# Running the first block's FFN as two half-batch passes, with their own loads, and products of a zero tile before them

## Chip, cores, metric

The kernel runs on one core of a Trainium2 chip. The metric is the device time of one execution in microseconds (us), the median of several runs. The span of a profile is about 2 us shorter, since it runs from the first to the last instruction. All runs quoted were classed fast, but for one run of the kernel before (246.25 us, named below), which was classed slow and is in no ratio; a one-core program has no second die to compare with.

## The reference, cut to what matters

A decayed linear attention over 4 batches, 8 heads, 768 positions and 64 dimensions (q, k, v), followed by a gated FFN on the 3072 x 512 result:

```python
# attention, block by block, with a state kv_state carried from block to block
out[:, :, sl] = intra + inter
kv_state = lam_block * kv_state + einsum('bhsd,bhse->bhde', kb_dec, vb)
...
gate = 1.0 / (1.0 + np.exp(-(x @ w_gate)))     # 512 -> 1536
val  = x @ w_val                               # 512 -> 1536
return (gate * val) @ w_out                    # 1536 -> 512
```

All inputs are float32 in HBM. The kernel converts them to bf16 while it loads them.

## The kernel before

The 768 positions are worked in six blocks of 128. A block is 4 batches x 128 positions = 512 tokens. TensorE gets a hand-made list of pieces. The ones that matter here are:

```python
def load(n, what, b0, b1):    # q, k, v of block n, batches b0..b1, by a queue that POOL fills
    ...
def load_gv(i, w):            # one sixth (256 columns) of w_gate and of w_val
    fs = slice(i * w, (i + 1) * w)
    nc.gpsimd.dma_start(out=WG[:, :, fs], in_=wg_r[:, :, fs])
    nc.gpsimd.dma_start(out=WV[:, :, fs], in_=wv_r[:, :, fs])

# piece_t: transposes of q and k     piece_s: scores     piece_m: score x mask -> MT (DVE)
# piece_a: products of MT and v, then the copy PSUM -> XT (XT is the FFN's input)
# piece_c: update of the state Sb

def piece_gv(n, ft):          # one of 12 column tiles of gate and value, 512 tokens
    for mt in range(NMT):     # 4 products, 512 columns
        nc.tensor.matmul(gp, lhsT=WG[:, mt, fs], rhs=x[:, mt, :], ...)
    nc.scalar.activation(sg, gp, AF.Sigmoid)
    for mt in range(NMT):
        nc.tensor.matmul(vp, lhsT=WV[:, mt, fs], rhs=x[:, mt, :], ...)
    nc.vector.tensor_mul(HT[n, ft], sg, vp)
...
piece_t(0, 0)                 # block 0: all attention first
piece_s(0, [0]); piece_m(0, 0)    # (one call per line in the kernel)
...
piece_a(0, [3])
units = gv[0] + gv[1][:4] + po[0] + gv[1][4:] + po[1]      # then the FFN
place(1, (2, 3), (8, 10), (9, 11), (11, 11))  # block 1's attention between block 0's FFN units
```

The four pairs of `place` are the FFN units after which the state update, the transposes, the scores and the products of v are put, one number for each pair of batches. The first loads, in queue order, are q and k of batches 0-1, q and k of batches 2-3, v of both halves, then the weight pieces 0 to 4, block 1's first q and k, and weight piece 5. From block 2 on, q and k are transposed by DMA instead of TensorE. SyncE issues those transposes in one instruction order with the output stores.

Of the kernel before, what the change touches and what calls it, by code (L numbers as in the profile page):

```python
# [8 lines left out]
FP32 = mybir.dt.float32  # L9
# [7 lines left out]
def kernel(  # L17
# [11 lines left out]
    nc = tc.nc  # L29
# [41 lines left out]
    def load(n, what, b0, b1):  # L71
        sl = slice(n * C, (n + 1) * C)
        for c in what:
            lst, src = {"q": (Q, q), "k": (K, k), "v": (V, v)}[c]
            if n not in lst:
                lst[n] = qkv.tile([128, B, H, D], BF16, tag=c + "b", name=c + "b")
            t = lst[n]
            nc.gpsimd.dma_start(  # L78
                out=t[:, b0:b1],
                in_=src[b0:b1, :, sl, :].rearrange("b h s d -> s (b h) d"))  # L80

    def load_gv(i, w):
# [3 lines that stand above are left out]
# [3 lines left out]
        nc.gpsimd.dma_start(out=WO[:, fs, :], in_=wo_r[:, fs, :])  # L89

    nc.scalar.preload_act_table_set("natural_log_exp_and_others")
    ident = const.tile([128, 128], BF16, tag="ident")
    make_identity(nc, ident)
    jn = const.tile([128, 2], FP32, tag="jn")
    ip1 = const.tile([128, C], FP32, tag="ip1")
    tri = const.tile([128, C], FP32, tag="tri")

    load(0, "q", 0, 2)
    for i, base in enumerate((-1, C - 1)):
        nc.gpsimd.iota(jn[:, i:i + 1], pattern=[[0, 1]], base=base, channel_multiplier=-1,  # L100
                       allow_small_or_imprecise_dtypes=True)
    load(0, "k", 0, 2)
    make_upper_triangular(nc, tri, val=1.0, diag=True)
    load(0, "q", 2, 4)
    nc.gpsimd.iota(ip1, pattern=[[1, C]], base=1, channel_multiplier=0,
                   allow_small_or_imprecise_dtypes=True)
    load(0, "k", 2, 4)
    load(0, "v", 0, 2)
    load(0, "v", 2, 4)


    Sb = stp.tile([128, B, HP, 128], BF16, tag="Sb", name="Sb")
    nc.vector.memset(Sb, 0.0)

    lnl = const.tile([128, H], FP32, tag="lnl")
    nc.scalar.activation(lnl, lam_bc, AF.Ln)
# [32 lines left out]
    def piece_t(n, bp):  # L149
        if n > 1:  # L150
            QS[n, bp] = trsb.tile([128, 2, HP, C], BF16, tag="QS", name="QS")
            nc.vector.tensor_tensor(out=QS[n, bp], in0=QR[n][:, 2 * bp:2 * bp + 2],  # L152
                                    in1=lamq.unsqueeze(1).to_broadcast([128, 2, HP, C]), op=ALU.mult)
            return
        tq = ps_at.tile([128, 2, HP, C], BF16, name="tq", tag="ps")
        tk = ps_at.tile([128, 2, HP, C], BF16, name="tk", tag="ps")
        for i in range(2):
            for hp in range(HP):
                nc.tensor.transpose(tq[:, i, hp, :], Q[n][:, 2 * bp + i, 2 * hp:2 * hp + 2, :], ident)  # L159
        QS[n, bp] = trsb.tile([128, 2, HP, C], BF16, tag="QS", name="QS")  # L160
        nc.vector.tensor_tensor(out=QS[n, bp], in0=tq,
                                in1=lamq.unsqueeze(1).to_broadcast([128, 2, HP, C]), op=ALU.mult)
        for i in range(2):
            for hp in range(HP):
                nc.tensor.transpose(tk[:, i, hp, :], K[n][:, 2 * bp + i, 2 * hp:2 * hp + 2, :], ident)  # L165
        KS[n, bp] = trsb.tile([128, 2, HP, C], BF16, tag="KS", name="KS")
        nc.scalar.copy(KS[n, bp], tk)  # L167
# [3 lines left out]
    def piece_s(n, bs):  # L171

        for b in bs:
            bp, i = b // 2, b % 2
            sp = [ps_at.tile([128, HP, C], FP32, name=f"sp{u}", tag="ps") for u in range(2)]
            for hp in range(HP):
                for u in range(2):
                    us = slice(u * 64, (u + 1) * 64)
                    nc.tensor.matmul(sp[u][:, hp, :], lhsT=KS[n, bp][us, i, hp, :],  # L179
                                     rhs=QS[n, bp][us, i, hp, :],  # L180
                                     start=(hp == 0), stop=(hp == HP - 1), skip_group_check=True)
            SP[n, b] = sp

    def piece_m(n, b):
        MT[n, b] = mtp.tile([128, 2, HP, C], BF16, tag="MT", name="MT")
        for u in range(2):
            nc.vector.tensor_tensor(out=MT[n, b][:, u], in0=SP[n, b][u], in1=mask[:, u], op=ALU.mult)  # L187

    def piece_a(n, bs):
        for b in bs:  # L190
            OP[n, b] = ps_at.tile([128, HP, C], FP32, name="op", tag="ps")
            for hp in range(HP if n > 0 else 0):
                nc.tensor.matmul(OP[n, b][:, hp, :], lhsT=Sb[:, b, hp, :],  # L193
                                 rhs=QS[n, b // 2][:, b % 2, hp, :],
                                 start=(hp == 0), stop=False, skip_group_check=True)
        for b in bs:
            for hp in range(HP):
                for u in range(2):
                    us = slice(u * 64, (u + 1) * 64)
                    nc.tensor.matmul(OP[n, b][us, hp, :], lhsT=V[n][:, b, 2 * hp + u, :],  # L200
                                     rhs=MT[n, b][:, u, hp, :],
                                     start=(n == 0 and hp == 0), stop=(hp == HP - 1),
                                     skip_group_check=True)
        if n not in XT:
            XT[n] = xtp.tile([128, NMT, B, C], BF16, tag="XT", name="XT")
        for b in bs:
            nc.scalar.copy(XT[n][:, :, b, :], OP[n, b])  # L207

    def make_kd(n):
        KD[n] = kdp.tile([128, B, H, D], BF16, tag="kd", name="kd")  # L210
        nc.gpsimd.tensor_tensor(  # L211
            out=KD[n], in0=K[n],
            in1=kds.unsqueeze(1).unsqueeze(3).to_broadcast([128, B, H, D]), op=ALU.mult)

    def piece_c(n, bs):
        for b in bs:
# [18 lines left out]

    HT = {}

    def piece_gv(n, ft):
        fs = slice(ft * 128, (ft + 1) * 128)
        x = XT[n].rearrange("p m b c -> p m (b c)")  # L240
        gp = ps_ff.tile([128, TCH], FP32, name="gp", tag="ff")
        for mt in range(NMT):
            nc.tensor.matmul(gp, lhsT=WG[:, mt, fs], rhs=x[:, mt, :],  # L243
                             start=(mt == 0), stop=(mt == NMT - 1))
        sg = htp.tile([128, TCH], BF16, tag="sg", name="sg", bufs=3)
        nc.scalar.activation(sg, gp, AF.Sigmoid)  # L246
        vp = ps_ff.tile([128, TCH], FP32, name="vp", tag="ff")
        for mt in range(NMT):
            nc.tensor.matmul(vp, lhsT=WV[:, mt, fs], rhs=x[:, mt, :],  # L249
                             start=(mt == 0), stop=(mt == NMT - 1))  # L250
        HT[n, ft] = htp.tile([128, TCH], BF16, tag="ht", name="ht", bufs=2 * NFT)
        nc.vector.tensor_mul(HT[n, ft], sg, vp)  # L252

    def piece_po(n, tt):
        po = ps_ff.tile([128, DM], FP32, name="po", tag="ff")
# [5 lines left out]
        nc.sync.dma_start(out=out[tt * S + n * C:tt * S + (n + 1) * C, :], in_=ob)  # L261


    for i in range(5):
        load_gv(i, DFF // 6)
    make_kd(0)
    load(1, "qk", 0, 2)
    load_gv(5, DFF // 6)
    load(1, "qk", 2, 4)
    load(1, "v", 0, 2)  # L270
    load(1, "v", 2, 4)
# [1 line left out]
        load_wo(i, NFT // 3)  # L273
    make_kd(1)


    piece_t(0, 0)
    piece_s(0, [0])
    piece_m(0, 0)
    piece_s(0, [1])  # L280
    piece_m(0, 1)
    piece_t(0, 1)
    piece_s(0, [2])
    piece_m(0, 2)
    piece_a(0, [0])
    piece_s(0, [3])
    piece_m(0, 3)
    piece_a(0, [1])
    piece_a(0, [2])
    piece_a(0, [3])  # L290

    gv = [[lambda n=n, ft=ft: piece_gv(n, ft) for ft in range(NFT)] for n in range(NSTEP)]
    po = [[lambda n=n, tt=tt: piece_po(n, tt) for tt in range(B)] for n in range(NSTEP)]

    units = gv[0] + gv[1][:4] + po[0] + gv[1][4:] + po[1]
    for n in range(2, NSTEP):
        units += gv[n] + po[n]
    start = {0: 0, 1: NFT}
    for n in range(2, NSTEP):
        start[n] = n * (NFT + B)  # L300
    after = [[] for _ in units]

    def place(n, c, t, s, a):


        for bp in range(2):
            bs = [2 * bp, 2 * bp + 1]
            after[c[bp]].append(lambda bs=bs: piece_c(n - 1, bs))
            after[t[bp]].append(lambda bp=bp: piece_t(n, bp))
            after[s[bp]].append(lambda bs=bs: piece_s(n, bs))  # L310
            after[s[bp]].append(lambda b=bs[0]: piece_m(n, b))
            after[s[bp] + (0 if s[bp] == NFT - 1 else 1)].append(lambda b=bs[1]: piece_m(n, b))
        for bp in range(2):
            bs = [2 * bp, 2 * bp + 1]
            after[a[bp]].append(lambda bs=bs: piece_a(n, bs))

    place(1, (2, 3), (8, 10), (9, 11), (11, 11))
    for n in range(2, NSTEP):
        u0 = start[n - 1] + (4 if n == 2 else 0)
        place(n, (u0, u0 + 1), (u0 + 2, u0 + 3), (u0 + 4, u0 + 7), (u0 + 8, u0 + 11))  # L320
# [40 lines left out]
```

## Time and profile before

| | |
|---|---|
| time | 241.31 us (3 runs, 241.28 to 241.86) |
| span | 239.2 us |
| TensorE busy | 93% of the span, 91% of the chain of waits |
| first FFN product | 19.46 us |
| block 1's FFN starts | 51.49 us |

From the page of the kernel before come the busy row of TensorE, the granted clock, and the DMA row. Each has 40 slices of 6 us, in tenths:

```profile
PE   0478999979999999999999999999999999999993
...
PEclk9995999999999999999999999999999999999999
DMA  7999999999999879971992650002950002100022
```

Two stretches are weak: the first four slices and the slice at 48 us. The clock is at half in slice 3. The page prints a 9 where the trace has no clock record yet, so the first slices are not evidence of a full clock. The DMA engines are busy from the start.

The waits of TensorE in the kernel before (engine, line, whom it waited for: total us, times, longest):

```profile
PE tq L159 <- DMA qb<-in_q_dram: 6.5, 1, 6.5
PE gp L243 <- ACT XT L207: 1.6, 2, 0.9
PE tk L165 <- DMA kb<-in_k_dram: 1.6, 1, 1.6
```

There is no wait for weights. The timeline of TensorE around the first FFN products (start us, duration us, engine, line, operation, count, idle time before):

```profile
19.46 1.87 PE L243 MATMUL gp<-XT,WG 128*128 128x512 bf16 x4 [0.67 <-ACT XT L207]
21.12 1.91 PE L249 MATMUL vp<-XT,WV 128*128 128x512 bf16 x4
22.83 1.91 PE L243 MATMUL gp<-XT,WG 128*128 128x512 bf16 x4
24.54 1.17 PE L249 MATMUL vp<-XT,WV 128*128 128x512 bf16 x4
```

Groups of four start 1.7 us apart here. Later in the same trace they start 0.86 us apart. That is the half clock, from 18.0 to 24.8 us, and it costs about 2.65 us.

When a load has landed is recorded in the trace, from the DMA queues to their semaphores. Half-loads of q, k or v land about 1.77 us apart, and 256 KB weight pieces 1.32 us apart.

### The profile page before, as it was taken

Reading aid. Unit: us, or ns where it says so; the run is one execution under the profiler, and the core shown is the slowest. Engines: PE = TensorE matmul, PEld = TensorE weight load, DVE = VectorE, ACT = ScalarE, POOL = GpSimd, SP = SyncE. Lnnn points to the kernel's source line nnn. Section 1 sums busy time; section 2 is a strip of 40 time slices with the busy share of each in tenths; the row PEclk is TensorE's granted clock in tenths of the full one; section 3 lists DMA queues with packets and bytes.
Section 4 is the critical chain, followed back from the end, with each engine's and each line's share of the span. In section 5 each row is a group of like instructions: output and inputs, shape, how many; then the busy total and the mean of one; then the engine's idle time right before and its main releaser. Section 6 shows DMA issues by size and latency. Waiting matters only on the chain.

```text
span 239.2 us, 3656 instructions
## 1 busy us (share of the span) xinstructions
PE 221.4 (93%) x1472; PEld 110.4 (46%) x1472; DVE 106.6 (45%) x181; ACT 78.9 (33%) x136; POOL 86.5 (36%) x72
## 2 busy tenths in 40 slices
PE   0478999979999999999999999999999999999993
PEld 0353545544544554544554544554544554444441
DVE  3381474844437720398620498520497510243300
ACT  3642224342122432222432223431223431323120
POOL 8969963903970990099300094000000000000000
PEclk9995999999999999999999999999999999999999
DMA  7999999999999879971992650002950002100022
GB/s 51 138 178 197 185 174 165 206 164 156 157 189 191 59 50 178 234 155 10 157 98 88 164 102 1 3 0 88 143 123 0 3 1 107 68 3 0 0 88 88
DMA packets 102288, 24.87 MB, mean 104 GB/s; under 512 B 91520, under 2 KB 99200, under 8 KB 102272
## 3 DMA queue, kind: packets, MB, share of 16 engines
q0 software_dynamic: 82032, 14.16, 77.3%
q1 hardware_dynamic: 20240, 10.49, 19.1%
q8 instruction: 11, 0.18, 0.3%
q14 instruction: 5, 0.04, 0.1%
HBM read 28.32 MB, written 6.29 MB: 145 GB/s over the span
## 4 chain that ended last, share of the span: by engine, by line
PE 91%; DMA 3%; ACT 2%; DVE 1%; issue 1%; POOL 0%; POOLq 0%; DVEq 0%
PE gp L243 27%; PE vp L249 26%; PE po L257 26%; DMA kb<-in_k_dram 3%; PE op L200 2%; PE cp L219 2%; PE op L193 2%; DVE MT L187 1%; PE tk L165 1%; ACT KS L167 1%; ACT XT L207 1%; PE tq L159 1%; PE sp_198 L179 0%; ACT ob L260 0%; POOL qb L78 0%
## 5 line engine op out<-in xcount | busy, mean ns | idle before, releaser
L252 DVE TENSOR_TENSOR ht<-sg,vp 128x512 bf16<-128x512 bf16 x72 | 49.5, 687 | 106.4 <-PE vp L249 105.6
L243 PE MATMUL gp<-XT,WG 128*128 128x512 bf16 x288 | 75.8, 386 | 1.6 <-ACT XT L207 1.6
L249 PE MATMUL vp<-XT,WV 128*128 128x512 bf16 x288 | 74.9, 383 | 0.0
L246 ACT ACTIVATE sg<-gp 128x512 bf16<-128x512 f32 x72 | 43.0, 597 | 82.8 <-PE gp L243 82.3
L257 PE MATMUL po<-WO,ht 128*128 128x512 bf16 x288 | 63.5, 379 | 0.0
L249 PEld LDWEIGHTS <-WV 128*128 128x128 bf16 x288 | 28.5, 99 | 35.0 <-issue 1.8
L257 PEld LDWEIGHTS <-ht 128*128 128x128 bf16 x288 | 27.8, 98 | 32.9
L243 PEld LDWEIGHTS <-WG 128*128 128x128 bf16 x288 | 27.0, 99 | 32.1 <-issue 3.4
L211 POOL TENSOR_TENSOR kd<-kb,kds 128x2048 bf16<-128x2048 bf16 x6 | 21.7, 3615 | 54.4 <-PE cp L219 33.9
L260 ACT COPY ob<-po 128x512 f32<-128x512 f32 x24 | 14.1, 586 | 50.0 <-PE po L257 50.0
L224 POOL TENSOR_TENSOR sd<-Sb,dec 128x512 f32<-128x512 bf16 x16 | 17.9, 1144 | 0.0
L207 ACT CAST XT<-op 128x512 bf16<-128x512 f32 x24 | 13.1, 588 | 13.6 <-PE op L200 13.6
L232 DVE TENSOR_TENSOR Sb<-cp,sd 64x256 bf16<-64x256 f32 x32 | 13.5, 421 | 4.1 <-POOL sd L224 3.0
L78 POOL DMA_DIRECT2D qb<-in_q_dram x8 | 11.9, 1488 | 0.1
L78 POOL DMA_DIRECT2D kb<-in_k_dram x8 | 11.5, 1442 | 0.0
L78 POOL DMA_DIRECT2D vb<-in_v_dram x8 | 11.4, 1440 | 0.0
L159 PE MATMUL tq<-ident,qb 128*128 128x128 bf16 x32 | 3.3, 265 | 6.5 <-DMA qb<-in_q_dram 6.5
L200 PE MATMUL op<-MT,vb 128*64 128x128 bf16 x192 | 8.4, 225 | 0.8 <-DVE MT L187 0.6
L193 PE MATMUL op<-QS,Sb 128*128 128x128 bf16 x80 | 6.4, 219 | 1.0 <-DVE MT L187 0.9
L200 PEld LDWEIGHTS <-vb 128*64 128x64 bf16 x192 | 6.2, 111 | 2.4 <-issue 1.1
L152 DVE TENSOR_TENSOR QS<-QR,lamq 128x1024 bf16<-128x1024 bf16 x8 | 7.2, 909 | 0.0
L193 PEld LDWEIGHTS <-Sb 128*128 128x128 bf16 x80 | 5.2, 98 | 3.4 <-issue 1.3
(129 smaller groups left out, 110.4 us busy)
## 6 DMA issues: line engine op xcount, KB each, us to landing
out_dram<-ob SPq DMA_DIRECT2D x24, 256.0 KB, 2.0
qb<-in_q_dram POOLq DMA_DIRECT2D x4, 512.0 KB, 8.1
kb<-in_k_dram POOLq DMA_DIRECT2D x4, 512.0 KB, 10.2
vb<-in_v_dram POOLq DMA_DIRECT2D x4, 512.0 KB, 13.3
WG<-in_moe_w_gate_dram POOLq DMA_DIRECT2D x6, 256.0 KB, 9.9
WV<-in_moe_w_val_dram POOLq DMA_DIRECT2D x6, 256.0 KB, 10.1
WO<-in_moe_w_out_dram POOLq DMA_DIRECT2D x3, 512.0 KB, 14.2
qb<-in_q_dram POOLq DMA_DIRECT2D x4, 256.0 KB, 7.4
```

The source lines that it names most:

```text
L78: nc.gpsimd.dma_start(out=t[:, b0:b1], in_=src[b0:b1, :, sl, :].rearrange("b h s d -> s (b h) d"))
L193: nc.tensor.matmul(OP[n, b][:, hp, :], lhsT=Sb[:, b, hp, :], rhs=QS[n, b // 2][:, b % 2, hp, :], start=(hp == 0), stop=False, skip_group_c ...
L200: nc.tensor.matmul(OP[n, b][us, hp, :], lhsT=V[n][:, b, 2 * hp + u, :], rhs=MT[n, b][:, u, hp, :], start=(n == 0 and hp == 0), stop=(hp == ...
L207: nc.scalar.copy(XT[n][:, :, b, :], OP[n, b])
L211: nc.gpsimd.tensor_tensor(out=KD[n], in0=K[n], in1=kds.unsqueeze(1).unsqueeze(3).to_broadcast([128, B, H, D]), op=ALU.mult)
L224: nc.gpsimd.tensor_tensor(out=sd, in0=Sb[:, b], in1=dec.unsqueeze(2).to_broadcast([128, HP, 128]), op=ALU.mult)
L243: nc.tensor.matmul(gp, lhsT=WG[:, mt, fs], rhs=x[:, mt, :], start=(mt == 0), stop=(mt == NMT - 1))
L246: nc.scalar.activation(sg, gp, AF.Sigmoid)
L249: nc.tensor.matmul(vp, lhsT=WV[:, mt, fs], rhs=x[:, mt, :], start=(mt == 0), stop=(mt == NMT - 1))
L252: nc.vector.tensor_mul(HT[n, ft], sg, vp)
L257: nc.tensor.matmul(po, lhsT=HT[n, ft][:, tt * 128:(tt + 1) * 128], rhs=WO[:, ft, :], start=(ft == 0), stop=(ft == NFT - 1))
L260: nc.scalar.copy(ob, po)
```

## The change

The intent is to start FFN work before all of block 0's attention is done. The q, k, v of batches 0-1 are loaded first, then weights, with the other three half-loads between them. Block 0's FFN runs in two passes, batches 0-1 and then 2-3. Each pass has twelve units of 256 columns. While TensorE waits for loads it multiplies a zero tile; the aim is that its clock is at full speed when the FFN begins. The diff, cut to its core:

```diff
     load(0, "q", 0, 2)
+    make_identity(nc, ident)
 ...
     load(0, "k", 0, 2)
-    load(0, "q", 2, 4)
-    load(0, "k", 2, 4)
     load(0, "v", 0, 2)
-    load(0, "v", 2, 4)
 ...
-    def piece_gv(n, ft):
+    def piece_gv(n, ft, b0=0, b1=B):            # tokens of batches b0..b1 only
 ...
-    for i in range(5):
+    for i in range(6):
+        if i in (2, 3, 4):
+            load(0, "qkv"[i - 2], 2, 4)
         load_gv(i, DFF // 6)
 ...
+    def warm(x):
+        wp = ps_ff.tile([128, TCH], FP32, name="wp", tag="ff")
+        for _ in range(x):
+            nc.tensor.matmul(wp, lhsT=Sb[:, 0, 0, :], rhs=Sb[:, 0], start=True, stop=True)
+    warm(9)
     piece_t(0, 0)
+    warm(3)
+    piece_s(0, [0, 1])
 ...
+    warm(3)
+    piece_a(0, [0, 1])
+    warm(2)
 ...
-    units = gv[0] + gv[1][:4] + po[0] + gv[1][4:] + po[1]
+    units = half[0] + half[1] + gv[1][:4] + po[0] + gv[1][4:] + po[1]
 ...
-    place(1, (2, 3), (8, 10), (9, 11), (11, 11))
+    place(0, None, (7,), (9,), (11,), (1,))     # batches 2-3 of block 0, inside pass one
+    place(1, (13, 14), (16, 18), (18, 20), (21, 23))
```

Also in the change, but cut here: the state tile Sb, which the zero products read, is cleared first of all; XT copies of odd batches of block 0 go to DVE instead of ScalarE, and the decayed k of block 0 is made in two halves.

More of the change, by code (lines that the diff above doesn't have):

```diff
@@ L91 @@
     nc.scalar.preload_act_table_set("natural_log_exp_and_others")
+    Sb = stp.tile([128, B, HP, 128], BF16, tag="Sb", name="Sb")
+    nc.vector.memset(Sb, 0.0)
     ident = const.tile([128, 128], BF16, tag="ident")
-    make_identity(nc, ident)
     jn = const.tile([128, 2], FP32, tag="jn")
@@ L102 @@
     load(0, "k", 0, 2)
-    make_upper_triangular(nc, tri, val=1.0, diag=True)
-    load(0, "q", 2, 4)
     nc.gpsimd.iota(ip1, pattern=[[1, C]], base=1, channel_multiplier=0,
                    allow_small_or_imprecise_dtypes=True)
-    load(0, "k", 2, 4)
+    make_upper_triangular(nc, tri, val=1.0, diag=True)
     load(0, "v", 0, 2)
-    load(0, "v", 2, 4)
-    Sb = stp.tile([128, B, HP, 128], BF16, tag="Sb", name="Sb")
-    nc.vector.memset(Sb, 0.0)
     lnl = const.tile([128, H], FP32, tag="lnl")
@@ L206, in piece_a, with make_kd @@
         for b in bs:
-            nc.scalar.copy(XT[n][:, :, b, :], OP[n, b])
-    def make_kd(n):
-        KD[n] = kdp.tile([128, B, H, D], BF16, tag="kd", name="kd")
+            if n == 0 and b % 2:
+                nc.vector.tensor_copy(XT[n][:, :, b, :], OP[n, b])
+            else:
+                nc.scalar.copy(XT[n][:, :, b, :], OP[n, b])
+    def make_kd(n, bps=(0, 1)):
+        if n not in KD:
+            KD[n] = kdp.tile([128, B, H, D], BF16, tag="kd", name="kd")
+        b0, b1 = 2 * bps[0], 2 * bps[-1] + 2
         nc.gpsimd.tensor_tensor(
-            out=KD[n], in0=K[n],
-            in1=kds.unsqueeze(1).unsqueeze(3).to_broadcast([128, B, H, D]), op=ALU.mult)
+            out=KD[n][:, b0:b1], in0=K[n][:, b0:b1],
+            in1=kds.unsqueeze(1).unsqueeze(3).to_broadcast([128, b1 - b0, H, D]), op=ALU.mult)
     def piece_c(n, bs):
@@ L236 @@
     HT = {}
-    def piece_gv(n, ft):
+    def piece_gv(n, ft, b0=0, b1=B):
         fs = slice(ft * 128, (ft + 1) * 128)
-        x = XT[n].rearrange("p m b c -> p m (b c)")
+        ts = slice(b0 * C, b1 * C)
+        w = (b1 - b0) * C
+        x = XT[n].rearrange("p m b c -> p m (b c)")[:, :, ts]
         gp = ps_ff.tile([128, TCH], FP32, name="gp", tag="ff")
         for mt in range(NMT):
-            nc.tensor.matmul(gp, lhsT=WG[:, mt, fs], rhs=x[:, mt, :],
+            nc.tensor.matmul(gp[:, :w], lhsT=WG[:, mt, fs], rhs=x[:, mt, :],
                              start=(mt == 0), stop=(mt == NMT - 1))
         sg = htp.tile([128, TCH], BF16, tag="sg", name="sg", bufs=3)
-        nc.scalar.activation(sg, gp, AF.Sigmoid)
+        nc.scalar.activation(sg[:, :w], gp[:, :w], AF.Sigmoid)
         vp = ps_ff.tile([128, TCH], FP32, name="vp", tag="ff")
         for mt in range(NMT):
-            nc.tensor.matmul(vp, lhsT=WV[:, mt, fs], rhs=x[:, mt, :],
+            nc.tensor.matmul(vp[:, :w], lhsT=WV[:, mt, fs], rhs=x[:, mt, :],
                              start=(mt == 0), stop=(mt == NMT - 1))
-        HT[n, ft] = htp.tile([128, TCH], BF16, tag="ht", name="ht", bufs=2 * NFT)
-        nc.vector.tensor_mul(HT[n, ft], sg, vp)
+        if (n, ft) not in HT:
+            HT[n, ft] = htp.tile([128, TCH], BF16, tag="ht", name="ht", bufs=2 * NFT)
+        nc.vector.tensor_mul(HT[n, ft][:, ts], sg[:, :w], vp[:, :w])
     def piece_po(n, tt):
@@ L261, in piece_po @@
         nc.sync.dma_start(out=out[tt * S + n * C:tt * S + (n + 1) * C, :], in_=ob)
-    for i in range(5):
+    for i in range(6):
+        if i in (2, 3, 4):
+            load(0, "qkv"[i - 2], 2, 4)
         load_gv(i, DFF // 6)
-    make_kd(0)
+        if i == 4:
+            make_kd(0, (0,))
     load(1, "qk", 0, 2)
-    load_gv(5, DFF // 6)
+    make_kd(0, (1,))
     load(1, "qk", 2, 4)
@@ L274 @@
     make_kd(1)
+    def warm(x):
[3 more added lines that the diff above has]
+    warm(9)
     piece_t(0, 0)
-    piece_s(0, [0])
+    warm(3)
+    piece_s(0, [0, 1])
     piece_m(0, 0)
-    piece_s(0, [1])
     piece_m(0, 1)
-    piece_t(0, 1)
-    piece_s(0, [2])
-    piece_m(0, 2)
-    piece_a(0, [0])
-    piece_s(0, [3])
-    piece_m(0, 3)
-    piece_a(0, [1])
@@ L289 @@
-    piece_a(0, [2])
-    piece_a(0, [3])
-    gv = [[lambda n=n, ft=ft: piece_gv(n, ft) for ft in range(NFT)] for n in range(NSTEP)]
+    warm(3)
+    piece_a(0, [0, 1])
+    warm(2)
+    gv = {n: [lambda n=n, ft=ft: piece_gv(n, ft) for ft in range(NFT)] for n in range(1, NSTEP)}
+    half = [[lambda b0=b0, ft=ft: piece_gv(0, ft, b0, b0 + NB2) for ft in range(NFT)]
+            for b0 in (0, NB2)]
     po = [[lambda n=n, tt=tt: piece_po(n, tt) for tt in range(B)] for n in range(NSTEP)]
-    units = gv[0] + gv[1][:4] + po[0] + gv[1][4:] + po[1]
+    units = half[0] + half[1] + gv[1][:4] + po[0] + gv[1][4:] + po[1]
@@ L296, with place @@
     for n in range(2, NSTEP):
         units += gv[n] + po[n]
-    start = {0: 0, 1: NFT}
-    for n in range(2, NSTEP):
-        start[n] = n * (NFT + B)
+    start = {n: NFT + n * (NFT + B) for n in range(2, NSTEP)}
+    start[1] = 2 * NFT
     after = [[] for _ in units]
-    def place(n, c, t, s, a):
-        for bp in range(2):
+    def place(n, c, t, s, a, bps=(0, 1)):
+        for i, bp in enumerate(bps):
             bs = [2 * bp, 2 * bp + 1]
-            after[c[bp]].append(lambda bs=bs: piece_c(n - 1, bs))
-            after[t[bp]].append(lambda bp=bp: piece_t(n, bp))
-            after[s[bp]].append(lambda bs=bs: piece_s(n, bs))
-            after[s[bp]].append(lambda b=bs[0]: piece_m(n, b))
-            after[s[bp] + (0 if s[bp] == NFT - 1 else 1)].append(lambda b=bs[1]: piece_m(n, b))
-        for bp in range(2):
+            if c:
+                after[c[i]].append(lambda bs=bs: piece_c(n - 1, bs))
+            after[t[i]].append(lambda bp=bp: piece_t(n, bp))
+            after[s[i]].append(lambda bs=bs: piece_s(n, bs))
+            after[s[i]].append(lambda b=bs[0]: piece_m(n, b))
+            after[s[i] + 1].append(lambda b=bs[1]: piece_m(n, b))
+        for i, bp in enumerate(bps):
@@ L314, in place @@
             bs = [2 * bp, 2 * bp + 1]
-            after[a[bp]].append(lambda bs=bs: piece_a(n, bs))
-    place(1, (2, 3), (8, 10), (9, 11), (11, 11))
+            after[a[i]].append(lambda bs=bs: piece_a(n, bs))
+    place(0, None, (7,), (9,), (11,), (1,))
+    place(1, (13, 14), (16, 18), (18, 20), (21, 23))
     for n in range(2, NSTEP):
```

## The prediction

> **What bounds the kernel now.** From 19.46 us on TensorE hardly stops: it is 91% of the chain of waits. Before, it is fed by loads: the timeline shows 6.5 us waiting for q, 1.6 us for k, then the serial path of transposes, scores, mask, products, copies. The clock row shows half clock from 18.0 to 24.8 us: about 12 FFN products start 0.43 us apart, later ones 0.216 us, which costs 2.65 us. A second hole: from 46.8 to 51.5 us TensorE has 1.9 us of work (waits for MT and XT). The DMA engines are busy nearly throughout from 4 to 60 us. The landings in the trace: half-loads of q, k, v finish about 1.77 us apart, 256 KB weight pieces 1.32 us apart; all six half-loads and ten of twelve weight pieces are in at 29.8 us.
>
> **What the change does.** It adds 17 zero products (the 9 before the first transpose take about 3.8 us), which fit into waits. It splits block 0's FFN into two passes of twelve units of 256 columns, with the same streaming time (0.86 us a unit at full clock). Loads: q, k, v of batches 0 and 1 first, then weights, with the other three loads between.
>
> The first half no longer waits for the second half's attention. I estimate q, k, v landed at 5.8, 8.9, 10.7 us and the first FFN product at 15.5 us. But pass one needs ALL gate and value weights, and the three other half-loads come before the last of them: 6 x 1.77 + 12 x 1.32 us of transfers from about 4.5 us puts the last weight piece at about 32 us (estimate). Before, it was not needed until 44 us. So pass one becomes DMA-bound. The last unit, products of batches 2 and 3 and the XT copy then put the start of pass two at about 34.6 us.
>
> Estimated sum: in the old kernel, after 19.46 us, without the cold penalty, 217.1 us remain; minus pass one's 10.4, 206.7 us after 34.6: 241.3 us. Minus 1.5 us: block 1's products now stand between short units (most of the hole goes). Plus 1 us: short units leave the three PSUM buffers half the time to be freed, while DVE does casts and masks. Plus 1 us: the starved pass lets the clock fall again. The Trainium skill (TensorE: Matmul & The Clock Gate, Part 1) says the clock is gated by activity in free-running 3.4 us windows; this trace agrees, its half-clock stretch is 6.83 us = 2 x 3.413. Span about 241.8 against 239.2 us.
>
> **Prediction: 243.5 us, range 240.0 to 247.0; faster by over 2%: 0.02; within 2%: 0.85; slower by over 2%: 0.13.** The earlier start is given back to the weight stream.
>
> **Signs.** Right: first FFN product near 15.5 us; TensorE busy 5 to 7 tenths from 19 to 33 us, with waits for WG and WV transfers in the table of waits (none before); pass two starts at 34 to 36 us; hole before block 1's FFN 1 to 1.5 us; from there on the old kernel, shifted. Wrong: no waits for WG/WV and pass two before 32 us (then faster); or full clock throughout (1 to 2 us better).
>
> **What would make it wrong.** Weights landing faster than 1.32 us a piece, or fewer gaps in the queue, moves the end one for one. Half clock for much of pass one puts pass two at 37 us and the time near 247. The DVE queue in pass two may cost more or nothing.

## The result, and the profile after

| | before | after |
|---|---|---|
| time, same rounds | 241.59 us (4 runs, 241.28 to 242.24) | 245.69 us (4 runs, 245.45 to 246.0) |
| span | 239.2 us | 243.9 us |
| first FFN product | 19.46 us | 15.18 us |
| last gate/value weight piece landed | 35.85 us | 32.9 us |
| start of pass two | none | 36.52 us |
| block 1's FFN starts | 51.49 us | 55.56 us |

The ratio is 1.0167 (95% interval 1.0139 to 1.0195). Ratios here are from the fast runs of both kernels in the same rounds, so they are not quite the ratio of the medians. The changed kernel is slower, by less than 2%.

The same rows of the page, after:

```profile
PE   6695679998999999999999999999999999999993
...
PEclk9869999999999999999999999999999999999998
DMA  7999999999999969990992390002590002200022
```

TensorE is now busy from 2 us on (zero products), but slices 3 to 5 are at 5, 6 and 7 tenths, where the old kernel had 8, 9 and 9. The waits of TensorE after name the reason:

```profile
PE gp L247 <- DMA WG<-in_moe_w_gate_dram: 2.8, 3, 1.8
PE vp L253 <- DMA WV<-in_moe_w_val_dram: 2.3, 4, 0.7
...
PE gp L247 <- DVE XT L204: 0.8, 1, 0.8
PE sp_2205 L175 <- DMA KR<-kb: 0.5, 1, 0.5
...
PE op L196 <- DVE MT L183: 0.4, 1, 0.4
```

The timeline of TensorE after shows pass one from its fifth unit, and its end:

```profile
19.91 0.61 PE L247 MATMUL gp<-XT,WG 128*128 128x256 bf16 x4 [0.32 <-DMA WG<-in_moe_w_gate_dram]
21.26 0.61 PE L253 MATMUL vp<-XT,WV 128*128 128x256 bf16 x4 [0.73 <-DMA WV<-in_moe_w_val_dram]
...
24.53 0.61 PE L247 MATMUL gp<-XT,WG 128*128 128x256 bf16 x4 [1.78 <-DMA WG<-in_moe_w_gate_dram]
25.87 0.61 PE L253 MATMUL vp<-XT,WV 128*128 128x256 bf16 x4 [0.73 <-DMA WV<-in_moe_w_val_dram]
...
32.95 0.61 PE L253 MATMUL vp<-XT,WV 128*128 128x256 bf16 x4 [0.16 <-DMA WV<-in_moe_w_val_dram]
33.40 0.60 PE L247 MATMUL gp<-XT,WG 128*128 128x256 bf16 x4
33.84 0.60 PE L253 MATMUL vp<-XT,WV 128*128 128x256 bf16 x4
34.37 0.62 PE L196 MATMUL op<-MT,vb 128*64 128x128 bf16 x9
35.34 0.38 PE L196 MATMUL op<-MT,vb 128*64 128x128 bf16 x7 [0.35 <-DVE MT L183]
36.52 0.61 PE L247 MATMUL gp<-XT,WG 128*128 128x256 bf16 x4 [0.79 <-DVE XT L204]
```

The first unit of the third, fourth and fifth weight piece stops for its gate weights and again for its value weights; that of the last piece stops for its value weights alone. The last value piece lands at 32.9 us, and 3.6 us later pass two begins. Those 3.6 us contain 1.3 us of FFN products. The rest is the attention of batches 2-3, with waits for a mask product (MT) and for the XT copy. The timeline of DVE in the same stretch shows why the second MT is late:

```profile
32.75 0.68 DVE L183 TENSOR_TENSOR MT<-sp_430,mask 128x512 bf16<-128x512 f32 x1
33.67 0.42 DVE L257 TENSOR_TENSOR ht<-sg,vp 128x256 bf16<-128x256 bf16 x1 [0.24 <-PE vp L253]
34.01 0.68 DVE L183 TENSOR_TENSOR MT<-sp_439,mask 128x512 bf16<-128x512 f32 x1
34.61 0.68 DVE L183 TENSOR_TENSOR MT<-sp_440,mask 128x512 bf16<-128x512 f32 x1
35.21 0.41 DVE L257 TENSOR_TENSOR ht<-sg,vp 128x256 bf16<-128x256 bf16 x1
35.77 0.69 DVE L204 CAST XT<-op 128x512 bf16<-128x512 f32 x1
```

These rows stand in the order of the program. The second pair of mask products (sp_439, sp_440) stands behind the FFN product of unit 10, which waits for the last value weights. The products with v, for their part, stand behind unit 11 in TensorE's own program order, so they could not begin before about 34.3 us whatever DVE did. So these masks, the products with v and the copy to XT all run after the last load, although q, k and v of batches 2-3 had landed by 27.5 us. Of the 3.6 us, the wait for MT is 0.35 us and the wait for XT 0.79 us.

### The profile page after: what moved, and what is told of

Its sections match the earlier page's. It is cut to its first block, busy times and chain, and to the rows that moved or that the text cites. A ratio compares the mean times of both kernels' runs of the same rounds, so it can differ in the third digit from the quotient of the medians.

```text
span 243.9 us, 3932 instructions
## 1 busy us (share of the span) xinstructions
PE 227.3 (93%) x1585; PEld 119.3 (49%) x1585; DVE 109.2 (45%) x195; ACT 79.7 (33%) x146; POOL 86.6 (35%) x73
## 4 chain that ended last, share of the span: by engine, by line
PE 79%; DMA 11%; POOL 5%; DVE 2%; issue 1%; ACT 1%; POOLq 0%; DVEq 0%
PE po L262 26%; PE gp L247 23%; PE vp L253 22%; DMA WV<-in_moe_w_val_dram 4%; DMA qb<-in_q_dram 4%; DMA KR<-kb 3%; PE op L196 2%; PE op L189 2%; PE cp L220 1%; DVE MT L183 1%; POOL WG L84 1%; POOL WV L85 1%; POOL kd L212 1%; DVE ht L257 1%; POOL qb L78 1%
## 5 line engine op out<-in xcount | busy, mean ns | idle before, releaser
L257 DVE TENSOR_TENSOR ht<-sg,vp 128x512 bf16<-128x512 bf16 (+1 forms) x84 | 51.2, 610 | 108.3 <-PE vp L253 106.7
L247 PE MATMUL gp<-XT,WG 128*128 128x512 bf16 (+1 forms) x336 | 76.6, 351 | 4.6 <-DMA WG<-in_moe_w_gate_dram 2.8
L253 PE MATMUL vp<-XT,WV 128*128 128x512 bf16 (+1 forms) x336 | 76.4, 350 | 2.5 <-DMA WV<-in_moe_w_val_dram 2.3
L250 ACT ACTIVATE sg<-gp 128x512 bf16<-128x512 f32 (+1 forms) x84 | 45.0, 536 | 88.5 <-PE gp L247 86.8
L253 PEld LDWEIGHTS <-WV 128*128 128x128 bf16 x336 | 32.7, 98 | 33.5 <-DMA WV<-in_moe_w_val_dram 3.4
L247 PEld LDWEIGHTS <-WG 128*128 128x128 bf16 x336 | 31.0, 98 | 32.8 <-DMA WG<-in_moe_w_gate_dram 3.5
L212 POOL TENSOR_TENSOR kd<-kb,kds 128x2048 bf16<-128x2048 bf16 (+1 forms) x7 | 21.9, 3128 | 58.2 <-PE cp L220 36.1
L206 ACT CAST XT<-op 128x512 bf16<-128x512 f32 x22 | 11.9, 588 | 13.8 <-PE op L196 13.8
L288 PE MATMUL wp<-Sb 128*128 128x512 bf16 x17 | 7.3, 583 | 2.0 <-DVE Sb L94 2.0
L220 PEld LDWEIGHTS <-kd 128*128 128x128 bf16 x80 | 5.3, 98 | 1.9
```

The costliest lines, as they stand in the source:

```text
L206: nc.scalar.copy(XT[n][:, :, b, :], OP[n, b])
L212: nc.gpsimd.tensor_tensor(out=KD[n][:, b0:b1], in0=K[n][:, b0:b1], in1=kds.unsqueeze(1).unsqueeze(3).to_broadcast([128, b1 - b0, H, D]), o ...
L247: nc.tensor.matmul(gp[:, :w], lhsT=WG[:, mt, fs], rhs=x[:, mt, :], start=(mt == 0), stop=(mt == NMT - 1))
L250: nc.scalar.activation(sg[:, :w], gp[:, :w], AF.Sigmoid)
L253: nc.tensor.matmul(vp[:, :w], lhsT=WV[:, mt, fs], rhs=x[:, mt, :], start=(mt == 0), stop=(mt == NMT - 1))
L257: nc.vector.tensor_mul(HT[n, ft][:, ts], sg[:, :w], vp[:, :w])
```

## Experiments

The theory was that pass two cannot start before all gate and value weights are in, so the end of pass one is set by the bytes ahead of the last weight piece and by what is chained behind it, not by how early pass one starts. The rivals were: the short units (half the time per PSUM buffer, into which the products are written, and more DVE work per unit of time) are slow by themselves; the zero products cost time; the mixed order of loads costs time. "Before" is run again beside each set. In the first set it had a median of 242.15 us (8 runs, one of them, 246.25 us, slow), in the second 241.84 (7 runs), in the third 243.05 (4 runs), and its fast runs went from 241.23 to 244.88 us. Most of the other kernels scatter by under 1.6 us. I therefore read medians and traces together, and no verdict below rests on a difference under 1 us alone.

### half_data: fewer bytes ahead of the last weight piece (wrong result)

```diff
+    def src(n, b):
+        return b % 2 if n == 0 else b       # used for every read of Q, K, V
 ...
-        if i in (2, 3, 4):
-            load(0, "qkv"[i - 2], 2, 4)
```

> Wrong result on purpose: the changed kernel, where block 0's batches 2 and 3 use the q, k, v of batches 0 and 1, so three half-loads (3 x 1.77 = 5.3 us of transfers) fall out ahead of the last weight piece. All instructions of the compute engines stay. Theory (pass two starts when the last weight piece is in): last piece at about 27.6 us in place of 32.9, pass two starts at about 31.3 in place of 36.5 us, time about 240.5 us (239.5 to 241.5). Rival (short units, PSUM buffers or DVE make pass one slow): pass two stays at 35 us or later, time above 244 us.

Measured: 240.53 us (240.15 to 241.47), ratio 0.9941 to before, with the wrong result. The last weight piece landed at 27.6 us, and pass two began at 31.23 us (TensorE's timeline in this run):

```profile
27.67 0.61 PE L256 MATMUL vp<-XT,WV 128*128 128x256 bf16 x4
...
31.23 0.61 PE L250 MATMUL gp<-XT,WG 128*128 128x256 bf16 x4 [0.79 <-DVE XT L207]
```

All three numbers are as the theory said. The compute instructions are the same, so the short units do not set the pace of pass one; the load queue does. The 3.6 us from the last piece to pass two stayed.

### attn_early: attention of batches 2-3 moved into the weight waits

```diff
-    place(0, None, (7,), (9,), (11,), (1,))
+    place(0, None, (5,), (7,), (9,), (1,))
```

> The changed kernel with the attention of batches 2 and 3 moved two units forward in pass one (transposes after unit 5, scores after 7, products after 9 in place of 7, 9, 11), where TensorE waits for weights anyway. Theory (1.7 to 2.2 us between the last weight piece and pass two are not transfer but a DVE queue: the second mask product stands behind the FFN product of unit 10, which waits for the last weight piece, then the products and the XT copy): pass two starts at about 34.4 in place of 36.5 us, time 243.6 us (243.0 to 244.3). Rival (only the transfer counts, the tail is hidden): 245 us or more.

Measured: 243.80 us (243.66 to 244.01), ratio 1.0071 to before. The last weight piece landed at 32.95 us as in the changed kernel. In TensorE's timeline the products with v now stand ahead of the last two units. Pass two (the last line below) follows those units without a gap, at 34.77 us:

```profile
31.72 0.62 PE L196 MATMUL op<-MT,vb 128*64 128x128 bf16 x9
32.70 0.38 PE L196 MATMUL op<-MT,vb 128*64 128x128 bf16 x7 [0.35 <-DVE MT L183]
33.02 0.61 PE L247 MATMUL gp<-XT,WG 128*128 128x256 bf16 x4
33.46 0.60 PE L253 MATMUL vp<-XT,WV 128*128 128x256 bf16 x4
33.90 0.60 PE L247 MATMUL gp<-XT,WG 128*128 128x256 bf16 x4
34.34 0.60 PE L253 MATMUL vp<-XT,WV 128*128 128x256 bf16 x4
34.77 0.60 PE L247 MATMUL gp<-XT,WG 128*128 128x256 bf16 x4
```

Pass two starts 1.75 us earlier and the time falls by 1.9 us. So about half of the change's loss of 4.1 us is this chain behind the last load, which needs no bytes to be moved. It needs only an order in which ready work does not stand behind work that waits for a load. The numbers were met, but not by the mechanism that I had written down, the DVE queue: the wait of 0.35 us for MT is still there (second line). What moved is TensorE's own order: the products with v and the copy to XT now come before the last two units, which had to wait for weights, and no longer after them. The edit moves DVE's work too, so no run separates the two orders; by the traces, DVE's part was at most 0.35 us.

### loads_first: same units, old order of loads

```diff
     load(0, "v", 0, 2)
+    load(0, "qkv", 2, 4)
 ...
-        if i in (2, 3, 4):
-            load(0, "qkv"[i - 2], 2, 4)
```

> The changed kernel with its own units and zero products, but with the load order of before: all six half-loads of block 0 first, then the weights. The first FFN product must wait for the first weights (about 18.5 us in place of 15.2), the last weight piece lands at the same 32 to 33 us since the bytes ahead of it are the same. Theory (the end of pass one is set by the bytes ahead of the last weight piece, not by the start): within 0.8 us of 245.7. Rival (the early start is worth its 3 us, or the mixed order of loads is what costs): off by 2 us or more, in either direction.

Measured: 245.32 us (245.15 to 245.89). The first FFN product came at 17.28 us, not 15.18, and the clock was at half until 23.2 us. Still the last weight piece landed at 32.95 us and pass two began at 36.56 us. An early start of pass one is worth nothing, and the mixed order of loads costs nothing. (The start at 18.5 us that I had expected was too late: it began with the gate weights at 17.2 us, while the value weights came at 18.55 us.)

### no_zeros: the change without zero products

```diff
-    warm(9)
     piece_t(0, 0)
-    warm(3)
 ...                       # and the other two
```

> The changed kernel without its 17 zero products. Theory: pass one waits for weights in any case, so the clock is worth little in it: within 1 us of 245.7 us, and the last weight piece lands at 32 to 33.5 us as before. Rival (zero products cost time by themselves): faster than 245 us by 1 us or more. Should pass two start at half clock, it would be up to 2 us slower.

Measured: 245.47 us (245.13 to 245.74), ratio 1.0138 to before. Full clock first came at 19.6 us, and it fell again from 26.4 to 29.9 us. Pass two began at 36.66 us. Within this change the zero products neither help nor harm.

The five kernels with two passes side by side (us):

| kernel | last weight piece | pass two starts | time | time minus start of pass two |
|---|---|---|---|---|
| after | 32.9 | 36.52 | 245.69 | 209.2 |
| no_zeros | 33.05 | 36.66 | 245.47 | 208.8 |
| loads_first | 32.95 | 36.56 | 245.32 | 208.8 |
| attn_early | 32.95 | 34.77 | 243.80 | 209.0 |
| half_data | 27.6 | 31.23 | 240.53 | 209.3 |

The last column is constant to 0.5 us (it mixes medians of different rounds with profiled runs; span minus start of pass two, from the profiled runs alone, is 206.8 to 207.4 us). Everything that moved the time moved the start of pass two.

### zeros_only: the old kernel with the zero products alone

```diff
+    warm(9)
     piece_t(0, 0)
+    warm(3)
 ...
     piece_t(0, 1)
+    warm(2)
 ...
     piece_a(0, [3])
+    warm(3)
```

> The kernel before with the 17 zero products alone (9, 3, 2 and 3 of them in TensorE's waits before the first FFN product), old loads, old full-width units. Theory (zero products are harmless and keep the clock; the loss of the change is the weight stream): the 12 half-clock FFN products at 19.5 to 24.8 us go to full clock, 2.65 us, and some transposes and scores of the first block run faster: 238.6 us, between 238.0 and 239.5. Rival (the zero products get in the way of the real ones, or do not hold the clock): 241 us or more.

Measured: 244.41 us (244.05 to 245.38), ratio 1.0109. The theory missed; the rival's number came, but not its reason. The gain was there: the first FFN products ran at full clock from 19.13 us, and block 1's FFN began at 48.50 us instead of 51.49. It was lost later: from there to the end this run took 193.8 us, the old kernel 187.7. The waits of TensorE in this run have a new first line, and its timeline shows the place:

```profile
PE sp L179 <- DMA KR<-kb: 4.5, 1, 4.5
```

```profile
103.06 1.03 PE L249 MATMUL vp<-XT,WV 128*128 128x512 bf16 x4
108.59 1.04 PE L179 MATMUL sp<-QS,KR 64*128 64x128 bf16 x16 [4.51 <-DMA KR<-kb]
109.56 0.61 PE L243 MATMUL gp<-XT,WG 128*128 128x512 bf16 x1
```

KR is block 3's k, transposed by DMA. SyncE's own timeline, first of zeros_only, then of the kernel before:

```profile
90.02 5.51 SPq L261 DMA_DIRECT2D out_dram<-ob  x3
95.63 5.50 SPq L144 DMA_TRANSPOSE QR<-qb  x1
101.22 5.24 SPq L144 DMA_TRANSPOSE KR<-kb  x1
```

```profile
95.60 2.92 SPq L261 DMA_DIRECT2D out_dram<-ob  x2
98.61 3.64 SPq L144 DMA_TRANSPOSE QR<-qb  x1
102.35 2.22 SPq L144 DMA_TRANSPOSE KR<-kb  x1
```

In the old kernel the transposes waited behind the stores until the loads of block 4 had nearly drained, took 3.6 and 2.2 us on SyncE, and k had landed at 106.65 us, only just before it was needed at 107.0 us. With TensorE 3 us ahead they were issued 3 us earlier, into those loads (a v load issued at 90.0 us landed at 106.7), and took 5.5 and 5.2 us. k landed at 108.55 us, later than in the kernel that was behind at this point. After the wait the clock was at half for 3.4 us as well; half of that, 1.7 us, and the 4.5 us of waiting make up about all of the 6.1 us lost. The Trainium skill (DMA: Bandwidth & Descriptors, "Issuing engines are not separate DMA queues") says that DMAs from all issuing engines end up on the same 16 DMA engines and interleave. These durations agree: beside the loads issued by POOL, the transposes issued by SyncE took 1.5 (q) and 2.4 (k) times as long.

### zeros_tr: the same, with the transposes issued ahead of the stores

```diff
-    loads = {start[n - 1]: n for n in range(2, NSTEP)}
+    loads = {start[n - 1] - (B if n > 2 else 0): n for n in range(2, NSTEP)}
```

Only SyncE's instruction order differs from zeros_only; the instruction lists of the other four engines are identical.

> The old kernel with zero products (the run zeros_only), and only the order on SyncE changed: the DMA transposes of q and k of a block are issued ahead of the four output stores of two blocks earlier, not behind them. Theory (zeros_only won 3 us at the start and lost 6 us in block 3, where the transposes, issued behind the stores at 95.6 us, met the loads of block 4 and took 5.4 us each, so TensorE waited 4.5 us for KR and its clock fell): the wait for KR goes, 238.6 us (237.8 to 239.4). Rival (the zero products themselves make the later part slower): 243 us or more, with waits elsewhere.

Measured: 237.96 us (237.75 to 238.16), ratio 0.9818. The wait for KR is gone from the list, and SyncE's timeline shows how:

```profile
73.93 5.64 SPq L144 DMA_TRANSPOSE QR<-qb  x1
79.69 4.80 SPq L144 DMA_TRANSPOSE KR<-kb  x1
87.04 8.10 SPq L261 DMA_DIRECT2D out_dram<-ob  x4
```

Block 3's transposes are as slow as in zeros_only, but k landed at 86.6 us, 17 us before it was needed at 103.6. So the zero products were not what cost time in zeros_only; the collision they triggered was.

### before_tr: the control

The old kernel with that one line alone.

> The old kernel with only the earlier transposes of the run zeros_tr, no zero products. Control: the old kernel has no wait of TensorE for KR, so theory: within 0.7 us of before. Rival (the early transposes are worth something by themselves): 1 us or more faster.

Measured: 240.46 us (239.26 to 240.80), ratio 0.9904 (0.9833 to 0.9976). That is 1.4 us under the median of before: by times alone the rival came true. The trace does not bear it out. Block 1's FFN began at 50.96 us, 0.5 us earlier than in the first profile of before, as the half clock ended at 23.9 instead of 24.8 us; from there to the end both took 187.7 us, so the earlier transposes, which are needed only after that point, gained nothing in it. zeros_tr took 187.7 us for the same part, too: in the profiles, all of its 3.4 us over before lie ahead of block 1's FFN. What the medians show beyond this is not explained; the scatter of before makes it hard to say. Against before_tr the gain of zeros_tr is 2.5 us, which is close to the 2.65 us that the half clock cost.

### zeros_tr_blk1 and zeros_tr_a: two tries to close the hole before block 1's FFN

```diff
-    place(1, (2, 3), (8, 10), (9, 11), (11, 11))
+    place(1, (2, 3), (7, 8), (8, 9), (10, 11))      # zeros_tr_blk1
+    place(1, (2, 3), (8, 10), (9, 11), (10, 11))    # zeros_tr_a
```

> The run zeros_tr with block 1's attention spread out: transposes after units 7 and 8, scores after 8 and 9, products after 10 and 11 (old: 8 and 10, 9 and 11, both 11). Theory: of the hole of 2.7 us before block 1's FFN about 1.1 us stays (the last XT copy), 1.3 to 1.6 us goes: 237.2 us (236.4 to 238.2), the best of all. Rival: the data of block 1 lands too late for it (q and k of its second half at about 38 to 40 us), no gain over zeros_tr.

> zeros_tr with one more move: the products of block 1's first two batches after unit 10 in place of 11, everything else of block 1 where it was. Transposes and scores stay where their loads are in, so the new load waits of zeros_tr_blk1 (1.9 us) do not come; the wait for MT ahead of the products (1.0 us) should go, the last XT copy (1.1 us) stays. Theory: 237.0 us (236.5 to 237.7). Rival (the move only shifts the wait to the scores, by PSUM buffers): within 0.4 us of zeros_tr.

Measured: zeros_tr_blk1 took 241.22 us (239.63 to 242.32), 3.3 us slower than zeros_tr, so the theory missed and the rival came true. In its timeline block 1's transposes now stop for q and k that have not landed, for 0.3 and 1.2 us (up to 39.1 us), and the scores stop 1.1 us for MT; the hole itself had shrunk to one idle gap of 0.9 us, as intended. The profiled run is the fastest of its four, 1.7 us over zeros_tr, and block 1's FFN begins 1.8 us later in it; the slower three were not profiled. zeros_tr_a took 239.7 us (238.8 to 241.15), 1.6 us slower. The wait for MT ahead of the products stayed (1.3 us in all), block 1's FFN began at 49.2 instead of 48.6 us, and the clock fell to half at 49.4 us for 3.4 us. (Both runs list a wait of 1.3 us of the scores for QS, but it stands in block 0, at about 14.7 us, ahead of anything that was moved; zeros_only has one of 1.1 us there.) The old placement was better than both.

### zeros_tr_5: the best kernel again

> The kernel of zeros_tr again, unchanged, in five rounds, because the runs of before scattered in the last call. Expected: 237.6 to 238.4 us, ratio 0.980 to 0.987 to before.

Measured: 238.14 us (6 runs, 237.69 to 238.35), ratio 0.9816 (0.9759 to 0.9874). That it is faster than before is clear of the noise; whether by over 2% is not, since the interval has 0.98 within it. It beats both kernels: 7.6 us under the changed one, 3.3 us under the fastest run of before in its own rounds (241.46).

## Why the prediction was right or wrong

**Right: the direction and the mechanism.** I expected a slower kernel within 2%, by a first pass that starts at 15.5 us (measured 15.18), then starves on the weight stream (waits for WG and WV in the list, TensorE at 5 to 7 tenths), so that the early start is given back. half_data and loads_first show it: the bytes ahead of the last weight piece set the time, and the start does not.

**Wrong: the size.** I predicted 243.5 us, 2.2 us over the 241.31 I had; measured were 245.69, 4.1 us over the 241.59 of the same rounds. In terms of the sum, in spans:

| term | predicted | measured |
|---|---|---|
| start of pass two | 34.6 us | 36.52 us |
| products after that, at full clock | 206.7 us | 206.7 us (taken over from the old trace) |
| hole before block 1's FFN and short units, together | -0.5 us | about 0 |
| clock | +1.0 us | 0 |
| after block 1's FFN began | 0 | +0.6 us |
| span | 241.8 us | 243.9 us (the terms add to 243.8) |

The step that failed is: "The last unit, products of batches 2 and 3 and the XT copy then put the start of pass two at about 34.6 us." It came at 36.52, and that is 1.9 of the 2.1 us by which the span was off. Half of the miss was the last weight piece, at 32.9 us instead of "about 32" (the sum as written there gives 31.0). The other half was what follows it: I allowed 2.6 us and it took 3.6. Of this 1.0 us, about 0.5 is that a weight piece serves two units, so the value products of unit 10 came after it as well as unit 11: 1.33 us of FFN products, where I had one unit of 0.86. Another 0.35 us is the wait for the mask products that stood in DVE's order behind the FFN product of unit 10. The rest, about 0.2 us, is not accounted for. attn_early gains 1.9 us, more than this miss, because it also hides products and a copy that I had counted as due after the last load.

The other terms were wrong too, but nearly cancelled (by +0.5, -1.0 and +0.6 us), which was luck. **The clock:** after 16.8 us it stayed at full speed in the starved pass, so my +1 us did not come. The Trainium skill (TensorE: Matmul & The Clock Gate, Part 1) describes a gate that follows activity in free-running windows of 3.4 us; this case agrees on the length of the windows (half-clock stretches of 3.41 and 6.83 us in several traces), but I could not predict from it which windows would be busy enough. Even at half clock it would have been hidden, as no_zeros and loads_first show. **Block 1's hole:** I expected most of it to go. The products were moved, but TensorE lost as much in many small gaps: start-to-start times beyond the streaming time add up to 3.3 us in the old trace from 24.7 to 51.5 us, and to 3.1 us in the new one from 36.5 to 55.6 us. I did not test this separately in the changed kernel. **The end:** a wait of 0.5 us for KR in block 5 is most of the +0.6 us, and is of the kind that zeros_only made large. The three traces with two passes that do not have it (attn_early, no_zeros, half_data) take 187.7 to 187.8 us from there to the end, as the old kernel does; the changed kernel takes 188.3.

**What stays open.** Why the fast runs of the old kernel scatter by up to 3.4 us within a later set while zeros_tr stays within 0.7 us is not shown; only one run of the old kernel was kept as a profile. Also open is why the median of before_tr lies about 1 us further below before than its trace explains.

## What to carry to other kernels

Before splitting a stage so that it can start earlier, ask what its first part needs in full: here the first half of the tokens needed all of the weights, so the end was fixed by bytes and the start was worth nothing. When a stage waits for a last load, look at every program order behind that load, TensorE's own first, and move ready work ahead of it. A gain at the start can also bring later transfers into collision; when a change makes one stage faster and the whole slower, look for the first wait that the old trace does not have.

## What the Trainium skill lacked or had wrong

- TensorE: Matmul & The Clock Gate, Part 4, says that full clock does not engage for transposes. In the changed kernel's trace, with the clock at full since 16.8 us, eight transposes take 0.45 us start to start (27.19 to 27.64 us), 56 ns each, as products of 128 columns do at full clock; at half clock, in the old trace from 6.5 us, they start 107 ns apart. So they run at full clock when other products have opened it. Whether transposes alone would open it, no run here shows.
- The same page, Part 1, does not say whether products of zeros open the clock gate. They can: in zeros_tr_5 the clock went to full at 4.7 us, when TensorE had run nothing but zero products since 2.0 us. In eight of the nine traces with zero products the first full clock came at 4.7 to 7.0 us, in no_zeros at 19.6 us. It is not certain, though: in attn_early the same nine products passed at half clock, and the first full clock came at 14.9 us; in the other eight it fell again for 3.4 or 6.8 us.
- The same page, Part 1, puts the ramp penalty at under 1% of a typical span. That figure is for the ramp, and half clock can cost more: here a later stretch of it, 18.0 to 24.8 us, after 3.4 us at full clock, cost about 2.65 of 239.2 us, or 1.1%.
- DMA: Bandwidth & Descriptors gives a transfer time by bytes, and no rate for loads that convert float32 to bf16. Here pieces of 512 KB read and 256 KB written land 1.32 us apart for weights (rows of 512 bytes written) and 1.77 us apart for q, k, v (128 bytes written).
- The same page gives a bandwidth for DMA transposes, and none for them beside loads. Here the transpose of block 3's k, 512 KB, took 2.2 us on SyncE and 4.3 us from issue to landing when the loads had landed, and 5.2 and 7.3 us beside the loads of one block.
